# Output tiles of one stage in other buffers, a block's pools in another order, and its TensorE work in program order

## The chip, the cores and the metric

One core of a Trainium2 chip runs the kernel. The metric is device time in microseconds: 888.29 us, the median of three runs (886.44, 888.29 and 888.67 us).

TensorE (PE) does the matmuls; their weights are loaded on a second row of the profile (PEld). VectorE is DVE, ScalarE is ACT, GpSimd is POOL, SyncE is SP. Matmuls write PSUM, which has eight banks; DVE and ACT read them. SP issues nearly all DMAs, ACT issues a few. Each engine runs its instructions in the order in which the program holds them, and an instruction that waits holds up those behind it on its engine.

## The reference

An attention with 4 batches, 8 heads, 576 positions and head dimension 64 (half of the heads see a local window of 32, half see positions of the same residue modulo 32) gives 2304 rows of 512. Two feed-forward layers follow:

```python
h = x @ w_in                      # 2304 x 512 by 512 x 2048
x = (h - np.tanh(h)) @ w_out      # 2048 x 512
xn = x / np.sqrt(np.mean(x * x, axis=-1, keepdims=True) + 1e-06) * rms_g
g = xn @ w_gate                   # 512 x 1536
silu = g * (1.0 / (1.0 + np.exp(-g)))
return (silu * (xn @ w_val)) @ w_out   # 1536 x 512
```

The weights come as 8-byte floats, activations as 4-byte floats.

## The kernel before, in words

Every matmul operand is held as a high and a low part in TensorE's rounded 32-bit format, so a product takes three matmuls (high by high, high by low, low by high).

**Weights.** A raw tile (128 x 512 of 8-byte floats, 512 KB) is loaded by SP (L175). ACT reads it twice (L184 into a `ct` tile, L186 into a `ca` tile), DVE merges the two (L196), ACT writes the high part (L203) and DVE the low part (L207). `Stream.step` loads ahead, converts weight i and splits weight i - 1. For the second layer `Store.plain` (L343) and `Store.to` (L362) also put the merged and the split weights back to DRAM, since a later stage reads them again.

**First layer.** The 2304 rows run in five groups of columns; the last group (g = 4) has 512. For each of 16 slices f of the hidden dimension `unit` issues the 12 matmuls of h, tanh (ACT, L854), h - tanh (DVE, L859), the high part of g (ACT, L865), its low part (DVE, L870) and, one or two slices later, the 12 matmuls of the output (`pe_x`) into four PSUM banks. The tiles `tg` and `g` rotate through three buffers each; there are 82 units in all, so the last unit's g lies in `g0` and the one two before it in `g1`. After the last slice `evac_x` scales the four banks by ACT (L890) and stores them to the DRAM tensor `x2d` (L896); in the last group ACT issues the stores, two to a bank, and the tiles are `tg` buffers.

**Between the layers.** `preps` reads `x2d` back, takes the mean square (TensorE sums it with a matrix of ones, ps_r), computes the reciprocal root on DVE (L999 to L1010) and scales (L1013); `conv` (L1027, L1046, L1047) makes the seven operands of a Strassen product. It is a generator, drawn three steps at a time by the last group and by the plain block.

**The plain block.** The first 256 rows of the second layer are computed in the plain way, while the last weights are still being converted. For each f of 12 (L1376 to L1387): the stream is moved on, the stores of earlier weights are issued, `pe_gv` does 12 matmuls of 256 columns for gate and 12 for val, ACT takes the Silu (L937), DVE multiplies (L938), ACT and DVE split the product (L940, L941), and `pe_o` does the six matmuls with w_out2 for f - 2. Gate uses two PSUM banks in turn, val two others, and every third f uses two of the banks of `ps_x`, where the first layer's last output stood. The weights of out2 are ready in DRAM (L166).

**The Strassen stage** follows for the other 2048 rows, two blocks of 1024 by six pairs of f. Each pair does seven products for gate and val, and `out` (L1163). Its first product stands in the program before the plain block's last `pe_o` (L1123 to L1125, L1395).

**What sets the order.** A planner orders each engine's instructions by priority, which is the place in the program unless `high_priority` raises it, and by its own estimate of when an instruction is ready. Inside `manual_schedule` the named engines keep the order of the program. SP keeps it from near the end of group 3 (L1309). TensorE keeps it in groups 1 to 3 (L1298, L1311), is free in the last group and the plain block, and keeps it again from L1391.

**Pools.** A pool is placed on top of the pools that are open. Per partition, the region of `poolA` holds `cvt` (ca and ct, 8 KB), `held` (12 slots of 4 KB for weights), `gp` (tg, 6 KB) and `ghl` (g, 12 KB), 74 KB in all. When it closes, `pbn` takes 40 KB from its start and the pools of `poolB` lie above. On the other side `poolR` (the read-back x of the first 256 rows, the root's temporaries s2 and rz, and `ct2`) closes at the same time, and above poolA's old region there is some free space and then the place of `poolR`. The four pools of `poolB` need 16, 12, 12 and 9 KB (tmp, cvt2, rawb, pb), 49 in all: 34 lie in the rest of poolA's region and 15 above it. With `reuse_waits="tile"` a new tile waits for the last users of just those old tiles that it overlaps.

Of the kernel before, what the change touches and what calls it, by code (L numbers as in the profile page):

```python
# [7 lines left out]
F32 = mybir.dt.float32  # L8
# [12 lines left out]
WS = 2.0 ** -8  # L21
# [13 lines left out]
def attn_moe_moe_kernel(  # L35
# [24 lines left out]
    nc = tc.nc  # L60
    B, _, NC, D = q_str.shape
# [4 lines left out]
    S = NC * W  # L66
# [3 lines left out]
    SUB = 256  # L70
    subs = [[(b, t + 64 * u) for u in range(4)] for t in (0, SUB) for b in range(B)]
    subs[B:B] = [[(b, 2 * SUB) for b in range(B)]]
    groups = [(0, 1), (2, 3), (4,), (5, 6), (7, 8)]
    width = [SUB * len(g) for g in groups]
    NG = len(groups)
# [5 lines left out]
    def runs(s):  # L81

        r = []
        for i, (b, t) in enumerate(subs[s]):
            if r and r[-1][0] == b and r[-1][1] + r[-1][2] == t:
                r[-1][2] += 64
            else:
                r.append([b, t, 64, 64 * i])
        return r
# [23 lines left out]
    cvt = poolA.enter_context(tc.tile_pool(name="cvt", bufs=2))  # L113
    held = poolA.enter_context(tc.tile_pool(name="held", bufs=HELD))
    gp = poolA.enter_context(tc.tile_pool(name="gp", bufs=1))
    ghl = poolA.enter_context(tc.tile_pool(name="ghl", bufs=1))
# [9 lines left out]
    for s in range(len(subs)):  # L126
        if len(runs(s)) > 1 or s in LANES:
            _, t0, n, _ = runs(s)[0]
            sc[t0] = one.tile([128, n // W, (t0 + n) // W], F32, name=f"sc{t0}")

    x2d = dram.tile([DM, NT], F32, name="x2d")
# [3 lines left out]
    def nth(tag, n):  # L135

        turn[tag] = (turn.get(tag, -1) + 1) % n
        return f"{tag}{turn[tag]}"
# [192 lines left out]
    xt, tmp = {}, [wts, None, None, None]  # L331

    class Store:


        n = m = 0
# [546 lines left out]
            evac_x(g)  # L883

    def evac_x(g):
        queue = nc.sync if g < NG - 1 else nc.scalar
        for c in range(4):
            pool, tag = (gp, nth("tg", 3)) if g == NG - 1 else (cvt, ("ca", "ct")[c % 2])
            t = pool.tile([128, 512], F32, tag=tag, name="xe")[:, :width[g]]
            nc.scalar.mul(out=t, in_=xacc[g][c][:, :width[g]], mul=WS)  # L890
            for k, j in enumerate(groups[g]):
                dst, src = x2d[c * 128:c * 128 + 128, :], t[:, SUB * k:SUB * k + SUB]
                rs = runs(j)
                b, t0, n, _ = rs[0]
                if len(rs) == 1:
                    queue.dma_start(out=dst[:, b * S + t0:b * S + t0 + n], in_=src)  # L896
                else:
                    queue.dma_start(
                        out=dst.rearrange("p (b t) -> p b t", b=B)[:, :, t0:t0 + n],
                        in_=src.rearrange("p (b t) -> p b t", b=B),  # L900
                    )
# [21 lines left out]
    def pe_gv(j, f):  # L923
        r, n = [], R0
        for kd, pool, tag in (("gate", ps_h, "h"), ("val", ps_m, "m")):
            if f % 3 == 2:
                ps = bank_x("ps_" + tag)[:, :n]
            else:
                ps = pool.tile([128, 512], F32, tag=nth(tag, 2), name="ps_" + tag)[:, :n]
            w, x = w2[kd, f].t, xn[j]  # L930
            seq = [(a, e, c) for c in range(4) for a, e in ((0, 0), (0, 1), (1, 0))]
            for i, (a, e, c) in enumerate(seq):
                mm(ps, w[:, a, c, :], x[:, e, c, :], i == 0, i == len(seq) - 1)
            r.append(ps)
        with tc.high_priority(400):
            s = pb.tile([128, n], F32, tag="s", name="s", bufs=3)
            nc.scalar.activation(out=s, in_=r[0], func=ACTF.Silu, scale=WS)  # L937
            nc.vector.scalar_tensor_tensor(out=s, in0=r[1], scalar=WS, in1=s, op0=ALU.mult, op1=ALU.mult)  # L938
            t = pb.tile([128, 2, n], F32R, tag="p", name="p", bufs=3)
            nc.scalar.copy(out=t[:, 0], in_=s)  # L940
            nc.vector.tensor_tensor(out=t[:, 1], in0=s, in1=t[:, 0].bitcast(F32), op=ALU.subtract)  # L941
        p_of[j, f] = t
# [423 lines left out]
    for k, m in enumerate((3, 7)):  # L1366
        xt[m] = late[:, 2048 * k:2048 * k + 4 * HT].rearrange("p (e c t) -> p e c t", e=2, c=2)
    poolB = ExitStack()
    tmp[0] = poolB.enter_context(tc.tile_pool(name="tmp", bufs=4, reuse_waits="tile"))
    tmp[1] = None  # L1370
    cvt = poolB.enter_context(tc.tile_pool(name="cvt2", bufs=2, reuse_waits="tile"))
    tmp[2] = cvt
    tmp[3] = (poolB.enter_context(tc.tile_pool(name="rawb", bufs=3, reuse_waits="tile")), "raw")
    pb = poolB.enter_context(tc.tile_pool(name="pb", bufs=2, reuse_waits="tile"))

    for f in range(FB):  # L1376
        if f == FB - 4:
            pairs[0].fetch((0, 1))
        st2.to(max(3 * (f + 2), N1 + (len(w2_order) - N1) * (f + 1) // (FB - 2)))
        store.plain(st2.i - 1)  # L1380
        store.to(st2.i - 6)
        pe_gv(0, f)
        for _ in range(3 if f < FB - 2 else 40):
            next(pg, None)
        decode.to(max(0, min(8, 8 * (f - 4) // 6)))
        if f > 1:
            pe_o(0, f - 2)  # L1387
    pe_o(0, FB - 2)
    store.plain(len(w2_order))
    store.to(len(w2_order))  # L1390
    ctx.enter_context(tc.manual_schedule(engines={mybir.EngineType.PE, mybir.EngineType.SP}))  # L1391

    def second():
# [149 lines left out]
```

## Time and profile before

| | |
|---|---|
| median of three runs | 888.29 us (886.44 to 888.67) |
| the profiled execution | 887.14 us |
| its span, first to last instruction | 885.3 us |
| mean granted TensorE clock | 0.99 of full speed |
| TensorE busy | 865.6 us, 98% |
| DVE busy | 626.1 us, 71% |
| ACT busy | 413.7 us, 47% |
| the last group's output leaves PSUM | 463.4 to 468.7 us |
| the plain block's last out2 products end | 523.4 us |

A busy share is a mean over stages with different limits. The stretch that the change touches is read in time order, from 455 to 525 us. In a timeline row the first two numbers are the start and the time in us, `x` is how many instructions are merged, and the bracket says how long the engine stood idle before and what it waited for.

### The profile page before, as it was taken

How to read it: one execution, taken by the hardware profiler on the slowest of the kernel's cores; microseconds unless marked ns; L12 is line 12 of the kernel's file. 1: busy time of each engine (PE TensorE's matmuls, PEld its weight loads, DVE VectorE, ACT ScalarE, POOL GpSimd, SP SyncE). 2: the span in 40 equal slices, each digit the busy share in tenths (PEclk: the TensorE clock that was granted, in tenths of full speed). 3: DMA queues.
4: the chain of work that ended last, by engine and by line, in shares of the span. 5: the costliest groups of instructions: out<-in, count | busy, mean ns of one | idle time of the engine just before them, and what ended most of it. 6: DMA issues, size and time to landing. Idle time of an engine off the chain costs nothing.

```text
span 885.3 us, 14070 instructions
## 1 busy us (share of the span) xinstructions
PE 865.6 (98%) x5091; PEld 723.4 (82%) x5091; DVE 626.1 (71%) x1290; ACT 413.7 (47%) x916; POOL 247.6 (28%) x309
## 2 busy tenths in 40 slices
PE   7999999999999999999997999999999999999998
PEld 4888888888998887888887977888888888888886
DVE  5999778888779887657779845469688553435544
ACT  6887633323543333778657544533325324322230
POOL 0000057694366853000000449956200000000000
PEclk7999999999999999999999999999999999999999
DMA  9965224221313000889976889866661289544002
GB/s 302 367 221 180 76 75 157 98 63 36 116 55 110 25 19 26 330 311 366 412 262 226 302 304 410 329 239 214 212 216 48 82 315 348 182 147 140 1 1 95
DMA packets 63749, 164.12 MB, mean 185 GB/s; under 512 B 10112, under 2 KB 21760, under 8 KB 63680
## 3 DMA queue, kind: packets, MB, share of 16 engines
q1 hardware_dynamic: 62528, 162.18, 52.2%
q10 hardware_dynamic: 1152, 1.05, 0.3%
q8 instruction: 40, 0.66, 0.3%
q14 instruction: 29, 0.24, 0.1%
HBM read 119.16 MB, written 44.04 MB: 184 GB/s over the span
## 4 chain that ended last, share of the span: by engine, by line
PE 60%; DVE 9%; POOL 7%; issue 2%; DMA 2%; ACT 1%; ACTq 0%; SPq 0%; DVEq 0%; POOLq 0%
PE ps_pr L150 21%; PE ps_o L150 15%; PE ps_x L150 9%; PE ps_h L150 9%; POOL pr L674 5%; DVE so L714 4%; PE ps_q L150 4%; PE ps_m L150 1%; POOL pr L707 1%; DMA raw<-in_w_val_dram 1%; DVE tg L859 1%; DVE g L870 1%; DMA x2d<-xe 1%; DVE sm L450 0%; DMA sq<-in_q_str_dram 0%
## 5 line engine op out<-in xcount | busy, mean ns | idle before, releaser
L150 PE MATMUL ps_h<-xs,w 128*128 128x512 f32 (+1 forms) x984 | 214.3, 366 | 0.7 <-DVE tg L859 0.7
L150 PE MATMUL ps_x<-g,w 128*128 128x512 f32 (+1 forms) x984 | 214.1, 366 | 0.0
L150 PEld LDWEIGHTS ps_h<-xs,w 128*128 128x128 f32 x984 | 169.7, 190 | 30.5 <-DVE tg L859 1.2
L150 PEld LDWEIGHTS ps_x<-g,w 128*128 128x128 f32 x984 | 168.5, 189 | 30.3 <-ACT g L865 0.4
L150 PE MATMUL ps_pr<-xt,wt 128*128 128x512 f32 x576 | 137.0, 390 | 0.5 <-DVE s L1096 0.5
L150 PE MATMUL ps_o<-wt,p 128*128 128x512 f32 x576 | 135.9, 389 | 0.0
L150 PEld LDWEIGHTS ps_pr<-xt,wt 128*128 128x128 f32 x576 | 107.9, 188 | 23.6 <-DVE s L1096 0.9
L150 PEld LDWEIGHTS ps_o<-wt,p 128*128 128x128 f32 x576 | 108.1, 188 | 22.4
L674 POOL TENSOR_TENSOR pr<-sk,sq 128x256 f32<-128x256 f32 (+2 forms) x101 | 83.1, 857 | 132.2 <-DMA sq<-in_q_str_dram 127.8
L865 ACT CAST g<-tg 128x512 fp32r<-128x512 f32 (+1 forms) x82 | 46.5, 567 | 101.2 <-DVE tg L859 100.9
L1117 ACT COPY u<-ps_pr 128x512 f32<-128x512 f32 x72 | 41.9, 587 | 102.8 <-PE ps_pr L150 102.8
L707 POOL TENSOR_TENSOR pr<-sv,se 128x288 f32<-128x288 f32 (+12 forms) x104 | 69.7, 691 | 57.4 <-DVE so L714 19.8
L1169 DVE SCALAR_TENSOR_TENSOR osum<-ps_o,osum 128x512 f32<-128x512 f32 x80 | 54.8, 687 | 26.6 <-PE ps_o L150 25.9
L714 DVE TENSOR_REDUCE so<-pr 128x16 f32<-128x272 f32 (+11 forms) x104 | 64.8, 651 | 8.9 <-POOL pr L707 8.6
L302 POOL TENSOR_TENSOR ws<-wa 128x256 f32<-128x256 f32 x24 | 20.4, 872 | 179.6 <-DVE w L207 155.6
L150 PE MATMUL ps_pr<-xt,wo 128*128 128x512 f32 x288 | 67.4, 389 | 0.0
L150 PEld LDWEIGHTS ps_pr<-xt,wo 128*128 128x128 f32 x288 | 54.1, 188 | 11.2
L870 DVE TENSOR_TENSOR g<-tg,g 128x512 fp32r<-128x512 f32 (+1 forms) x82 | 55.2, 674 | 10.4 <-ACT g L865 9.8
L859 DVE SCALAR_TENSOR_TENSOR tg<-ps_h,tg 128x512 f32<-128x512 f32 (+1 forms) x82 | 50.5, 617 | 15.8 <-ACT tg L854 15.8
L196 DVE SCALAR_TENSOR_TENSOR ct<-ca,ct 128x512 uint32<-128x512 uint32 x68 | 47.5, 706 | 18.9 <-ACT ca L186 18.4
L854 ACT ACTIVATE tg<-ps_h 128x512 f32<-128x512 f32 (+1 forms) x82 | 44.2, 540 | 35.5 <-PE ps_h L150 35.4
L679 DVE TENSOR_REDUCE sc<-pr 128x4 f32<-128x256 f32 (+2 forms) x101 | 43.7, 436 | 12.1 <-POOL pr L674 11.6
(123 smaller groups left out, 1041.1 us busy)
## 6 DMA issues: line engine op xcount, KB each, us to landing
wt<-w SPq DMA_DIRECT2D x84, 512.0 KB, 4.6
w<-w SPq DMA_DIRECT2D x36, 512.0 KB, 6.2
raw<-in_w_out_dram SPq DMA_DIRECT2D x28, 512.0 KB, 6.1
w<-wo SPq DMA_DIRECT2D x24, 512.0 KB, 7.1
raw<-in_w_in_dram SPq DMA_DIRECT2D x16, 512.0 KB, 9.2
raw<-in_w_gate_dram SPq DMA_DIRECT2D x12, 512.0 KB, 7.0
raw<-in_w_val_dram SPq DMA_DIRECT2D x12, 512.0 KB, 7.4
v<-ct SPq DMA_DIRECT2D x24, 256.0 KB, 5.3
```

The lines of the kernel that those rows point to most:

```text
L150: nc.tensor.matmul(out_, lhsT, rhs, start=start, stop=stop, skip_group_check=True)
L196: nc.vector.scalar_tensor_tensor(out=t, in0=self.a.bitcast(U32), scalar=3, in1=t, op0=ALU.logical_shift_left, op1=ALU.bitwise_or)
L674: nc.gpsimd.tensor_tensor(out=pr, in0=self.k[:, a:e, :], in1=self.q[:, c - c0:c - c0 + 1, :].to_broadcast([128, e - a, D]), op=ALU.mult,)
L679: pend.append(lambda: nc.vector.tensor_reduce(out=s[:, c - c0, a:e], in_=pr, axis=AX.X, op=ALU.add))
L707: nc.gpsimd.tensor_tensor(out=pr, in0=self.v[:, 0:c + 1, a:e], in1=self.e[:, c - c0, 0:c + 1].unsqueeze(2).to_broadcast([128, c + 1, e - a ...
L714: pend.append(lambda: nc.vector.tensor_reduce(out=o[:, c - g0, a:e], in_=pr.rearrange("l c d -> l d c"), axis=AX.X, op=ALU.add))
L854: nc.scalar.activation(out=t, in_=h_of[g, f, a], func=ACTF.Tanh, scale=WS)
L859: nc.vector.scalar_tensor_tensor(out=t, in0=h_of.pop((g, f, a)), scalar=WS, in1=t, op0=ALU.mult, op1=ALU.subtract)
L865: nc.scalar.copy(out=t[:, 0], in_=t_of[g, f, a])
L870: nc.vector.tensor_tensor(out=t[:, 1], in0=t_of.pop((g, f, a)), in1=t[:, 0].bitcast(F32), op=ALU.subtract)
L1117: nc.scalar.copy(out=u, in_=x[kd])
L1169: nc.vector.scalar_tensor_tensor(out=o, in0=ps, scalar=WS, in1=o, op0=ALU.mult, op1=ALU.add)
```

## The change

In the last group `evac_x` scales the four banks into two tiles with the tags g0 and g1, two banks to a tile, and issues one store for each half of the columns and each tile: four stores of 256 KB in place of eight of 128 KB. The pools of `poolB` are opened in the order rawb, tmp, pb, cvt2 in place of tmp, cvt2, rawb, pb. From f = 3 of the plain block TensorE keeps the order of the program; this ends after the block's loop, where the existing block for TensorE and SP begins.

```diff
--- before.py
+++ after.py
@@ -883,19 +883,27 @@
             evac_x(g)
 
     def evac_x(g):
-        queue = nc.sync if g < NG - 1 else nc.scalar
+        if g == NG - 1:
+            for h in range(2):
+                t = ghl.tile([128, 2, 512], F32, tag=("g0", "g1")[h], name="xe")
+                for c in range(2):
+                    nc.scalar.mul(out=t[:, c], in_=xacc[g][2 * h + c], mul=WS)
+                for k, j in enumerate(groups[g]):
+                    b, t0, n, _ = runs(j)[0]
+                    dst = x2d[256 * h:256 * h + 256, b * S + t0:b * S + t0 + n].rearrange("(c p) t -> p c t", p=128)
+                    nc.scalar.dma_start(out=dst, in_=t[:, :, SUB * k:SUB * k + SUB])
+            return
         for c in range(4):
-            pool, tag = (gp, nth("tg", 3)) if g == NG - 1 else (cvt, ("ca", "ct")[c % 2])
-            t = pool.tile([128, 512], F32, tag=tag, name="xe")[:, :width[g]]
+            t = cvt.tile([128, 512], F32, tag=("ca", "ct")[c % 2], name="xe")[:, :width[g]]
             nc.scalar.mul(out=t, in_=xacc[g][c][:, :width[g]], mul=WS)
             for k, j in enumerate(groups[g]):
                 dst, src = x2d[c * 128:c * 128 + 128, :], t[:, SUB * k:SUB * k + SUB]
                 rs = runs(j)
                 b, t0, n, _ = rs[0]
                 if len(rs) == 1:
-                    queue.dma_start(out=dst[:, b * S + t0:b * S + t0 + n], in_=src)
+                    nc.sync.dma_start(out=dst[:, b * S + t0:b * S + t0 + n], in_=src)
                 else:
-                    queue.dma_start(
+                    nc.sync.dma_start(
                         out=dst.rearrange("p (b t) -> p b t", b=B)[:, :, t0:t0 + n],
                         in_=src.rearrange("p (b t) -> p b t", b=B),
                     )
@@ -1366,12 +1374,12 @@
     for k, m in enumerate((3, 7)):
         xt[m] = late[:, 2048 * k:2048 * k + 4 * HT].rearrange("p (e c t) -> p e c t", e=2, c=2)
     poolB = ExitStack()
+    tmp[3] = (poolB.enter_context(tc.tile_pool(name="rawb", bufs=3, reuse_waits="tile")), "raw")
     tmp[0] = poolB.enter_context(tc.tile_pool(name="tmp", bufs=4, reuse_waits="tile"))
+    pb = poolB.enter_context(tc.tile_pool(name="pb", bufs=2, reuse_waits="tile"))
+    cvt = poolB.enter_context(tc.tile_pool(name="cvt2", bufs=2, reuse_waits="tile"))
     tmp[1] = None
-    cvt = poolB.enter_context(tc.tile_pool(name="cvt2", bufs=2, reuse_waits="tile"))
     tmp[2] = cvt
-    tmp[3] = (poolB.enter_context(tc.tile_pool(name="rawb", bufs=3, reuse_waits="tile")), "raw")
-    pb = poolB.enter_context(tc.tile_pool(name="pb", bufs=2, reuse_waits="tile"))
 
     for f in range(FB):
         if f == FB - 4:
@@ -1379,6 +1387,9 @@
         st2.to(max(3 * (f + 2), N1 + (len(w2_order) - N1) * (f + 1) // (FB - 2)))
         store.plain(st2.i - 1)
         store.to(st2.i - 6)
+        if f == 3:
+            order = ctx.enter_context(ExitStack())
+            order.enter_context(tc.manual_schedule(engines={mybir.EngineType.PE}))
         pe_gv(0, f)
         for _ in range(3 if f < FB - 2 else 40):
             next(pg, None)
@@ -1388,6 +1399,7 @@
     pe_o(0, FB - 2)
     store.plain(len(w2_order))
     store.to(len(w2_order))
+    order.close()
     ctx.enter_context(tc.manual_schedule(engines={mybir.EngineType.PE, mybir.EngineType.SP}))
 
     def second():
```

## Rows read from the trace of the kernel before

**Rows 1.** The page, part 1: busy us, share of the span, instructions.

```profile
PE 865.6 (98%) x5091; PEld 723.4 (82%) x5091; DVE 626.1 (71%) x1290; ACT 413.7 (47%) x916; POOL 247.6 (28%) x309
```

**Rows 2.** TensorE's waits: line waited for, total us, times, longest us.

```profile
PE ps_h L150 <- ACT s L937: 4.9, 1, 4.9
PE ps_s L150 <- DMA dq<-in_near_d_dram: 1.5, 1, 1.5
...
PE ps_pr L150 <- DVE s L1096: 0.5, 1, 0.5
```

**Rows 3.** Timeline, TensorE, 455 to 495 us.

```profile
461.59 2.91 PE L150 MATMUL ps_x<-g,w 128*128 128x512 f32 x12
...
466.47 3.04 PE L150 MATMUL ps_m<-xn,w 128*128 128x256 f32 x24
...
474.45 4.45 PE L150 MATMUL ps_h<-xn,w 128*128 128x256 f32 x24 [4.94 <-ACT s L937]
```

**Rows 4.** Timeline, ACT and its DMA issues, 455 to 495 us.

```profile
463.40 1.09 ACT L890 ACTIVATE xe<-ps_x 128x512 f32<-128x512 f32 x2 [3.29 <-PE ps_x L150]
...
465.24 0.69 ACT L998 ACTIVATE acc<-ps_r,cole 128x512 f32<-128x512 f32 x1 [0.26 <-PE ps_r L150]
465.30 2.79 ACTq L896 DMA_DIRECT2D x2d<-xe  x4
...
468.13 0.60 ACT L890 ACTIVATE xe<-ps_x 128x512 f32<-128x512 f32 x1 [2.21 <-DMA x2d<-xe]
...
472.16 0.76 ACT L184 ACTIVATE ct<-raw,colf 128x512 uint32<-128x512 uint16 x1 [3.43 <-DMA x2d<-xe]
...
474.03 0.90 ACT L937 ACTIVATE s<-ps_h 128x256 f32<-128x256 f32 x3
```

**Rows 5.** Windows of 2 us: busy by engine, granted clock (PEclk), DMA.

```profile
474.00:476.00 2.00, 1.55 (x7) 1.55 (x8) 2.00 (x6) 2.00 (x6) 0.00 (x0) 0.51 0.16 59
476.00:478.00 2.00, 2.00 (x13) 2.00 (x13) 1.77 (x3) 2.00 (x4) 0.00 (x0) 0.63 0.20 76
478.00:480.00 2.00, 2.00 (x19) 2.00 (x18) 2.00 (x2) 2.00 (x3) 0.00 (x0) 1.00 0.87 272
```

**Rows 6.** Window of 25 us: the same columns.

```profile
475.00:500.00 25.00, 25.00 (x174) 23.75 (x173) 24.77 (x39) 21.08 (x38) 1.05 (x2) 0.95 0.78 265
```

**Rows 7.** Timeline, SP's DMA issues, 455 to 546 us.

```profile
474.87 3.05 SPq L343 DMA_DIRECT2D v<-ct  x2
...
508.13 0.39 SPq L175 DMA_DIRECT2D raw<-in_w_val_dram  x1
```

**Rows 8.** Timeline, TensorE and ACT, 494 to 546 us.

```profile
505.85 1.53 PE L150 MATMUL ps_x<-w,p 128*128 128x512 f32 x6
...
513.51 1.52 PE L150 MATMUL ps_pr<-xt,wt 128*128 128x512 f32 x6
...
515.33 1.60 PE L150 MATMUL ps_h<-xn,w 128*128 128x256 f32 x12
515.87 0.77 ACT L184 ACTIVATE ct<-raw,colf 128x512 uint32<-128x512 uint16 x1 [3.22 <-DMA raw<-in_w_val_dram]
...
516.76 1.55 PE L150 MATMUL ps_pr<-xt,wt 128*128 128x512 f32 x6
...
518.62 0.51 PE L150 MATMUL ps_m<-xn,w 128*128 128x256 f32 x2 [0.32 <-ACT w L203]
...
521.76 1.65 PE L150 MATMUL ps_x<-w,p 128*128 128x512 f32 x6 [0.95 <-ACT p L940]
```

**Rows 9.** The tile xe: ns of one issue, min/median/max.

```profile
L896 ACTq DMA_DIRECT2D x2d<-xe x8: 326/368/692, 464.0 to 469.1; - x8
L898 SPq DMA_DIRECT2D x2d<-xe x4: 583/616/1657, 279.9 to 282.9; - x4
```

**Rows 10.** DMA issues: count, KB, median us to landing.

```profile
x2d<-xe ACTq DMA_DIRECT2D x8, 128.0 KB, 3.6
```

**Rows 11.** Timeline, DVE, 455 to 495 us.

```profile
465.96 0.43 DVE L999 TENSOR_SCALAR sq<-acc 128x512 int32<-128x512 int32 x1 [5.12 <-ACT acc L998]
```

## Prediction

> **What bounds the kernel now.** I read the busy shares first: TensorE is busy for 865.6 of 885.3 us [rows 1], so no edit here can win more than the idle time that it removes, some 20 us in all, and the clock that goes with it. Then the list of TensorE's waits over the whole run, longest first: one wait of 4.9 us for ACT's Silu (L937) stands alone, the next is 1.5 us, and the only one listed for the Strassen products that follow is 0.5 us [rows 2]. Then the same place in order of time. TensorE ends the last group's output matmuls at 464.5, runs on into the plain block, ends the third pair of gate and val products at 469.5 and stands until 474.45, because the bank that it needs next is read by the first Silu [rows 3]. ACT shows why the Silu is late: it scales the four accumulators of the last group into three tg buffers, so the fourth waits 2.21 us for the first output DMA to land; it issues all eight output DMAs itself; and the conversion at 472.16 waits 3.43 us more, because its tile lies where the tg buffers were [rows 4]. The Silu follows at 474.03.
>
> The 2 us windows show a second cost of the same stop: the granted clock is 0.51 and 0.63 of full speed in the two windows after it and 1.00 again from 478 [rows 5]. The busy time of those windows, 1.55 and 2.00 us, at those shares, is a loss of 0.76 + 0.74 = 1.5 us.
>
> The other half of the block has another limit. The weights pass through a ring: SP loads a raw tile, ACT and DVE convert it, SP stores the result and only then comes to the next load. From 475 to 500 DVE is busy for 24.77 of 25 us and ACT for 21.08 [rows 6]. The last raw tile (val, f = 11) is loaded at 508.13, ACT gets it at 515.87, TensorE runs its products from 518.62, and the block's last out2 products end at 521.76 + 1.65 = 523.4 [rows 7, 8]. TensorE was kept busy up to there by work taken out of order: the first Strassen product (12 matmuls, at 513.51 and 516.76) goes before val 11, though it comes after it in the program [rows 8].
>
> **The change part by part.** The sum is made against the profiled execution, 885.3 us of span and 887.14 us in all, 1.15 us under the median of 888.29; I subtract the same microseconds from the median.
>
> *Output tiles.* Four ACT scalings stay. They go into g0 and g1, two to a buffer, so the wait of 2.21 us goes [rows 4]. g0 holds the last unit's g (82 units, three buffers, so the last is g0), and all twelve matmuls of that unit read it: the scaling of c = 0 can start at 464.5 instead of 463.40, 1.1 us later [rows 3, 4]. Four scalings at 0.55 us end at 466.7. Eight DMA issues on ACT's queue become four. Four of the old ones stand in one row of 2.79 us, 0.70 each with what lies between them [rows 4]; the issue alone is 326 to 692 ns, median 368 [rows 9]. A new one covers 256 rows of DRAM instead of 128. So four take 1.5 us at the old median, 2.8 at the 0.70; the nearest row of a larger pattern, the four-run store of the middle group (median 616 ns) [rows 9], says 2.5, and I take that. With 0.7 us for the norm's scaling, which stands among them now too, ACT is through at 464.5 + 2.2 + 0.7 + 2.5 = 469.9, and the last pair is issued between 468 and then.
>
> *The pools.* By the sizes, the region that closes holds ca/ct 8 KB, held 48, tg 6, g 12. Before, the plain block's ct and ca tiles began on tg; now rawb takes three slots of held, the temporaries take held's last slot, tg, g0 and half of g1, pb (the Silu's s and p) takes the rest of g1, g2 and free space, and ct/ca lie on the right side's closed pools. So the conversion that waited 3.43 us waits for no output DMA. But two of the three s tiles lie on g1, so a Silu can wait for the second output pair to land. The landing takes 3.6 us in the median on that queue [rows 10]: issued at 468 to 469.9, it has landed at 471.6 to 473.5. If the first s tile is the one on g2 it waits for nothing and the Silu runs at about 469.8. Ends: the stop of 4.94 us goes nearly whole, or only 474.03 - 473.5 = 0.5 us of it does. I take 472.0 for the Silu, 2.0 us before 474.03, nearer the landing rows, because the tiles of a pool are taken in turn and the lowest is on g1. The conversions that stood ahead of the Silu (472.16 to 474.03, 1.9 us) can run in that wait. TensorE started 0.4 us after the Silu did [rows 3, 4]; so the stop ends at 472.4 and shrinks by 2.0 us. I take 2.2, since four fewer transfers share the queue.
>
> *The clock.* A stop of 2.7 us instead of 4.94 brings back between nothing and all of the 1.5 us [rows 5]; I take half, 0.8.
>
> *Program order from f = 3.* It adds no instruction. It takes away TensorE's freedom to fill a wait. In order, val 11 is followed by two out2 steps (f = 9 and 10), the first Strassen product and out2 of f = 11. By their rows, val takes 1.6 us, an out2 step of six 1.5, the twelve Strassen matmuls 3.1: after val 11's weight arrives 1.6 + 1.5 + 1.5 + 3.1 + 1.5 = 9.2 us, against 523.4 - 518.6 = 4.8 us now [rows 8]; less 0.15 us of overlap per step, 8.5. So the order costs 3.7 us if TensorE still waits for that weight, 0.6 if the Strassen product may still go ahead (its own block of program order did pass unordered work before), and nothing if the weights come 3.7 us sooner. What can bring them: SP stood behind the stop too; its first store of the block waited until 474.87, and the later loads stand behind it [rows 7]. With the first conversion 2 to 4 us sooner that store can go at 471 to 473. Against it: DVE idles 5.12 us before 465.96, which the change doesn't touch, and has no gap from there to 500 [rows 6, 11]. I take the ring to gain what the order loses, net nothing, with -2 and +3.7 as ends.
>
> The Trainium skill, "TensorE: Matmul & The Clock Gate", section "Loop structure matters more than you think", speaks against this part: whether the array stays at full clock depends on whether the program makes it wait between bursts. The trace agrees: after the one stop the windows show 0.51 and 0.63. By that rule an in-order wait as long as today's stop would take back 1.5 us of clock beside its own length, and the sum would be 1.5 us instead of 3.0.
>
> Sum: 2.2 + 0.8 + 0 = 3.0 us. On the profiled execution 884.1, on the median 885.3. After 523 TensorE has almost no idle time [rows 2], so I let the gain stand to the end.
>
> **The rivals.** *A, the forecast*: 885.3.
>
> *B, the ring hides it*: the stop shrinks, but val 11 still arrives at 518 because DVE is full, and TensorE waits there instead; the Strassen product may go ahead. For it: DVE's 24.77 of 25 us, and ACT's wait of 3.22 us for the last load [rows 6, 8]. Against it: ACT and SP were idle behind the stop, so some links move. Time: 888.3 + 0.6, less 1 us if the ring moves by half of the Silu's 2 us: 887.9.
>
> *C, the order blocks the end*: program order puts out2 9 and 10 and the Strassen product behind val 11. Price 3.7 us, and up to 1.5 us of clock if the wait before it is as long as today's stop; it decides if the ring gains less than about 1 us. Time 888.3 + 3.7 = 892, with the front's gain swallowed by the wait. For it: the fill at 513.51 and 516.76 [rows 8]. Against it: one front gain of 2 us in the ring halves it.
>
> *D, the pools don't free the Silu*: its s tile waits for the second pair up to 473.5. Then 0.5 us is won and the rest is as in B: 887.8. It goes with B.
>
> *E, the whole stop goes* and the ring follows: 4.94 + 1.5 = 6.4 us, 881.9. It goes with the faster side.
>
> **How the numbers follow.** About 0.3%, 2.7 us, is what can be told from no change. A and E together 0.42, of which E 0.10; B and D 0.31; C 0.27. A by itself lies between 883.5 and 887, so part of it could not be told from no change (under 885.6 it could); about as much of B falls under that line, so I leave faster 0.42, same 0.31, slower 0.27. The likeliest case gives 885.3. The range that holds 8 in 10 reaches from E's side, 881.8, to C, 892.
>
> **What would show it.** The step on the output tiles: four scalings back to back after 464.5, no wait between them for an output DMA, four issues under 0.75 us each. The pools: no conversion that waits for an output DMA, and the first Silu at about 472; at 469.8 E is right, after 473 D. The clock: one window or none under 0.9 after the stop. The order: the first Strassen product after val 11 or before it; TensorE's waits for w (L203, L207) between 500 and 520, under 1 us in all for A, over 3 us for C. The ring: the load of the last raw tile before 506 for A, at 507 to 508 for B. The prediction is wrong if the block's last out2 products end later than 523.4, or if TensorE's stop at 469.5 is as long as before.

## The result: slower, and the profile after

The changed kernel takes 893.85 us (median of 7 runs, 892.12 to 897.8) against 888.4 us before (7 runs, 886.44 to 889.3): ratio 1.0070, 95% interval 1.0047 to 1.0093, so it is slower by 0.5 to 0.9%. Forecast was 885.3, range 881.8 to 892.0. Some executions of e2, e4, e8 and e9 below, and one of the kernel before beside e9 to e11, took 1440 us and more; medians and ratios leave them out, and the profiled executions of e8 and e9 were such ones, so the table of the runs has no row for these two.

The profiled execution took 896.41 us, span 894.6 (before 887.14 and 885.3). So the two profiles lie 9.3 us apart and the medians 5.45: the profiled execution after is one of the slower ones of its kernel (mean granted clock 0.985; the fastest, 892.12 us, had 0.992), and what is read off the pair is more than the usual loss. Behind the edit of the output tiles every line number is 8 higher, so the Silu is L945.

The whole run's TensorE waits, to be read against [rows 2] (line waited for, total us, times, longest us): the Silu's wait is shorter, as foreseen, and a second one, for DVE's half of p, is new.

```profile
PE ps_x L150 <- DVE p L949: 3.7, 1, 3.7
PE ps_h L150 <- ACT s L945: 3.4, 1, 3.4
...
PE ps_pr L150 <- DVE s L1104: 1.1, 1, 1.1
```

ACT's timeline after, against [rows 4]. The output tiles did what was forecast: four scalings in a row, four issues. Then ACT stands 5.75 us at the Silu, whose tile lies on g1, until the output has landed, and the first conversion, which waits for nothing, comes behind it and three more Silus at 476.88 (before: 472.16).

```profile
464.56 2.31 ACT L890 ACTIVATE xe<-ps_x 128x512 f32<-128x512 f32 x4 [3.74 <-PE ps_x L150]
466.42 0.39 ACTq L894 DMA_DIRECT2D x2d<-xe  x1
...
466.84 1.60 ACTq L894 DMA_DIRECT2D x2d<-xe  x3
473.20 0.94 ACT L945 ACTIVATE s<-ps_h 128x256 f32<-128x256 f32 x3 [5.75 <-DMA x2d<-xe]
...
476.88 0.76 ACT L184 ACTIVATE ct<-raw,colf 128x512 uint32<-128x512 uint16 x1
```

SP's timeline, against [rows 7]: the ring's first store is 8.1 us later, its last raw load 5.6 (0.7 of it because all that lies ahead ended 0.7 later).

```profile
482.93 2.06 SPq L343 DMA_DIRECT2D v<-ct  x2
...
513.77 0.43 SPq L175 DMA_DIRECT2D raw<-in_w_val_dram  x1
```

TensorE's timeline, against [rows 3] and [rows 8]: two stops, val 11 at 524.21 instead of 518.62, and 18 out2 matmuls behind it instead of 6, ending at 526.23 + 4.27 = 530.50 (before 523.41). The Strassen product at 518.55 did go ahead of gate 11.

```profile
473.63 2.93 PE L150 MATMUL ps_h<-xn,w 128*128 128x256 f32 x12 [3.42 <-ACT s L945]
...
497.52 2.08 PE L150 MATMUL ps_x<-w,p 128*128 128x512 f32 x4 [3.72 <-DVE p L949]
...
518.55 1.63 PE L150 MATMUL ps_pr<-xt,wt 128*128 128x512 f32 x6 [0.37 <-DMA wt<-w]
...
524.21 0.51 PE L150 MATMUL ps_m<-xn,w 128*128 128x256 f32 x2
...
526.23 4.27 PE L150 MATMUL ps_x<-w,p 128*128 128x512 f32 x18
```

The 2 us windows, against [rows 5], columns as there (window, length, PE, PEld, DVE, ACT, POOL busy, granted clock, DMA): around the end of each stop stand four windows with a granted clock of 0.50 to 0.74. Busy time times what is missing of the clock gives 2.7 us for either set, 5.5 in all; before it was 1.5.

```profile
472.00:474.00 2.00, 0.37 (x1) 0.37 (x2) 0.39 (x2) 0.80 (x3) 0.00 (x0) 0.58 0.31 108
474.00:476.00 2.00, 2.00 (x11) 2.00 (x11) 2.00 (x7) 1.14 (x4) 0.00 (x0) 0.50 0.00 0
476.00:478.00 2.00, 2.00 (x11) 2.00 (x11) 0.90 (x2) 1.40 (x3) 0.00 (x0) 0.50 0.00 0
478.00:480.00 2.00, 2.00 (x11) 1.83 (x10) 0.77 (x2) 1.42 (x3) 0.00 (x0) 0.71 0.00 0
496.00:498.00 2.00, 0.48 (x1) 0.48 (x2) 2.00 (x4) 0.75 (x3) 0.00 (x0) 0.56 1.02 355
498.00:500.00 2.00, 2.00 (x7) 1.61 (x7) 2.00 (x5) 0.86 (x2) 0.00 (x0) 0.50 0.77 272
500.00:502.00 2.00, 2.00 (x12) 2.00 (x11) 2.00 (x4) 1.74 (x3) 0.00 (x0) 0.50 1.01 345
502.00:504.00 2.00, 2.00 (x14) 2.00 (x14) 2.00 (x4) 1.89 (x4) 0.00 (x0) 0.74 0.71 231
```

TensorE's second stop, of 3.72 us, is a wait for DVE, which does 2.35 us of preparations ahead of p's low part:

```profile
494.78 2.35 DVE L1055 TENSOR_TENSOR xt<-tr,xt 128x1024 fp32r<-128x1024 f32 x2
497.05 0.42 DVE L949 TENSOR_TENSOR p<-s,p 128x256 fp32r<-128x256 f32 x1
```

DVE, which was full from 465.96 to 500 before [rows 6, 11], now stands 2.07 us for the Silu and 2.33 us for val's matmuls, which TensorE runs at half clock. The first merge of a weight comes at 482.22 (before: 474.16), though its conversion was done at 477.53 + 0.67 = 478.20: the waiting product and the chain's four scalings stand ahead of it.

```profile
473.61 1.09 DVE L946 SCALAR_TENSOR_TENSOR s<-ps_m,s 128x256 f32<-128x256 f32 x3 [2.07 <-ACT s L945]
...
479.23 0.42 DVE L946 SCALAR_TENSOR_TENSOR s<-ps_m,s 128x256 f32<-128x256 f32 x1 [2.33 <-PE ps_m L150]
...
482.22 0.69 DVE L196 SCALAR_TENSOR_TENSOR ct<-ca,ct 128x512 uint32<-128x512 uint32 x1
```

The same 15 us from the end of the output matmuls, DVE alone (window, length, busy, clock, DMA), first after, then before (464 to 479): 4.6 us less work done.

```profile
465.00:470.00 5.00, 2.42 (x4) 1.00 0.58 138
470.00:475.00 5.00, 2.86 (x7) 0.73 0.49 177
475.00:480.00 5.00, 2.67 (x7) 0.58 0.00 0
sum 15.00, DVE 7.95; mean DVE 2.65
```

```profile
sum 15.00, DVE 12.54; mean DVE 4.18
```

Where the 9.3 us between the two profiled spans lie: 0.7 ahead of the block, 6.4 in it (from the start of the last output matmul, 464.81 against 464.11, to the end of the last out2: 65.7 against 59.3), 2.0 behind it and 0.2 after the last matmul. The start is chance: over all runs below that matmul starts between 461.1 and 465.1, as TensorE stands and loses clock by different amounts in the stages before it. So only times from it on are compared. Of the 6.4, 1.95 is more standing (gaps between matmuls 8.38 against 6.43) and the other 4.4 the same 342 matmuls run slower (4.0 of it by the clock, 5.5 against 1.5). The medians being 5.45 apart, these shares are those of this pair and not of every execution.

### The profile page after: what moved, and what is told of

The parts are those of the page before. It is cut to its first block, busy times and chain, and to the rows that moved or that the text cites. A ratio compares the mean times of both kernels' runs of the same rounds, so it can differ in the third digit from the quotient of the medians.

```text
span 894.6 us, 14061 instructions
## 1 busy us (share of the span) xinstructions
PE 869.8 (97%) x5091; PEld 725.8 (81%) x5091; DVE 628.8 (70%) x1290; ACT 413.8 (46%) x916; POOL 245.0 (27%) x309
## 4 chain that ended last, share of the span: by engine, by line
PE 71%; DVE 12%; POOL 7%; DMA 4%; issue 3%; ACT 2%; SPq 1%; ACTq 0%; DVEq 0%; POOLq 0%
PE ps_pr L150 20%; PE ps_h L150 16%; PE ps_x L150 15%; PE ps_o L150 14%; POOL pr L674 5%; DVE so L714 4%; PE ps_q L150 4%; DMA raw<-in_w_in_dram 1%; DMA raw<-in_w_gate_dram 1%; POOL pr L707 1%; PE ps_v L150 1%; PE ps_s L150 1%; PE ps_p L482 1%; DVE tg L859 1%; DVE g L870 1%
## 5 line engine op out<-in xcount | busy, mean ns | idle before, releaser
L707 POOL TENSOR_TENSOR pr<-sv,se 128x288 f32<-128x288 f32 (+12 forms) x104 | 70.2, 695 | 56.3 <-DVE so L714 19.8
L1177 DVE SCALAR_TENSOR_TENSOR osum<-ps_o,osum 128x512 f32<-128x512 f32 x80 | 54.8, 687 | 26.9 <-PE ps_o L150 26.3
L870 DVE TENSOR_TENSOR g<-tg,g 128x512 fp32r<-128x512 f32 (+1 forms) x82 | 55.3, 675 | 10.8 <-ACT g L865 9.6
L679 DVE TENSOR_REDUCE sc<-pr 128x4 f32<-128x256 f32 (+2 forms) x101 | 43.7, 437 | 12.1 <-POOL pr L674 11.6
```

The source lines that it names most:

```text
L679: pend.append(lambda: nc.vector.tensor_reduce(out=s[:, c - c0, a:e], in_=pr, axis=AX.X, op=ALU.add))
L707: nc.gpsimd.tensor_tensor(out=pr, in0=self.v[:, 0:c + 1, a:e], in1=self.e[:, c - c0, 0:c + 1].unsqueeze(2).to_broadcast([128, c + 1, e - a ...
L870: nc.vector.tensor_tensor(out=t[:, 1], in0=t_of.pop((g, f, a)), in1=t[:, 0].bitcast(F32), op=ALU.subtract)
L1177: nc.vector.scalar_tensor_tensor(out=o, in0=ps, scalar=WS, in1=o, op0=ALU.mult, op1=ALU.add)
```

## The experiments

Theory 1: the pools put a wait for the output's landing at the head of ACT's queue, and the conversions stand behind it, so the ring runs late. Theory 2: program order on TensorE costs by itself. The times of the block in each profiled run, read from the timelines, in us behind the start of the last output matmul (last two columns: length of the block, and from its end to the last matmul). Each row is one execution, and a difference of a microsecond or two may be chance: the profiled execution of e6 (890.89) lies 5.0 us under its kernel's median, that of e13 (884.28) 3.9 under, that of the changed kernel 2.6 over.

| run | first conversion | first Silu | last weight's high part | val 11 | block | behind it |
|---|---|---|---|---|---|---|
| before | 8.1 | 9.9 | 53.8 | 54.5 | 59.3 | 358.3 |
| after | 12.1 | 8.4 | 58.7 | 59.4 | 65.7 | 360.3 |
| e1 tiles, pools | 13.8 | 8.4 | 58.7 | 59.4 | 66.2 | 360.0 |
| e2 order | 7.0 | 8.8 | 51.9 | 56.7 | 65.2 | 358.0 |
| e3 pools | 8.7 | 0.7 | 56.8 | 57.5 | 62.3 | 360.4 |
| e4 tiles | 3.7 | 11.5 | 49.1 | 52.6 | 61.0 | 360.3 |
| e5 | 3.7 | 9.4 | 53.5 | 57.8 | 62.0 | 360.4 |
| e6 (order) | 3.7 | 9.4 | 52.8 | 57.9 | 66.3 | 357.8 |
| e7 order from 6 | 7.2 | 9.0 | 53.4 | 54.7 | 60.4 | 359.6 |
| e10 | 2.5 | 5.0 | 52.2 | 56.3 | 60.6 | 359.9 |
| e11 (order) | 3.7 | 6.1 | 53.0 | 58.3 | 66.9 | 359.2 |
| e12 | 7.0 | 8.8 | 53.6 | 54.8 | 59.4 | 360.3 |
| e13 | 2.5 | 5.0 | 51.0 | 53.7 | 57.9 | 358.8 |
| e14 (order) | 11.3 | 8.5 | 59.5 | 60.1 | 68.7 | 360.2 |
| e15 | 8.7 | 0.7 | 54.0 | 55.3 | 60.5 | 359.3 |
| e16 | 8.3 | 1.1 | 60.1 | 61.0 | 65.5 | 360.0 |
| e17 | 1.9 | 7.3 | 53.1 | 53.8 | 58.9 | 359.3 |
| e18 (order) | 1.9 | 8.6 | 53.5 | 56.6 | 62.3 | 359.4 |

**The parts alone.** The kernel before with one or two hunks of the change's diff: e1 the output tiles and the pools, e2 the order, e3 the pools, e4 the output tiles.

> The change without the program order on TensorE: output tiles and pools as changed, TensorE free. Theory 1 (the first Silu's tile lies on g1, so ACT waits for the output DMA with the weight conversions queued behind it, and the weight ring starts late): almost the whole loss stays, 4 to 6 us slower than before; ACT's wait for the output DMA about 5.7 us, SP's first merged-weight store of the block about 8 us later than before. Theory 2 (program order on TensorE is what costs): within 1 us of before, or faster.

> Only the program order on TensorE from f = 3; tiles and pools as before. Theory 1: the ring starts as before (first store near 475), the last weight arrives as before, and the end of the block is at most 1.5 us later: 0 to 2 us slower. Theory 2: 4 to 6 us slower, with TensorE waits of several us between 490 and 520.

> Only the pools in the new order; the output tiles stay in tg with eight stores, TensorE free. The first Silu's tile lies on g1, which no output uses now. Theory 1: the Silu waits for no output DMA, TensorE's stop of 4.9 us shrinks to under 1 us, and the ring starts no later than before: 1 to 4 us faster. Theory 2 says nothing against it: 0 to 3 us faster. A third possibility, that the new places of the conversion tiles alone delay the ring: 2 to 5 us slower.

> Only the output tiles through g0 and g1 with four stores; pools and TensorE's freedom as before. Conversion tiles lie on tg, which no output uses now, except one on g0; the Silu's tile lies on the closed pools of the other side. Theory 1: no long wait of ACT for an output DMA ahead of the first conversion, which starts by 469; ring 3 to 4 us earlier; 1 to 4 us faster. Theory 2: 0 to 3 us faster. If half the stores change nothing: within 1 us.

Measured, with the kernel before at 887.27 beside them: e1 894.36, ratio 1.0077 (1.0048 to 1.0106); e2 892.22, 1.0055 (1.0037 to 1.0072); e3 891.32, 1.0042 (1.0021 to 1.0062); e4 890.96, 1.0033 (1.0014 to 1.0052). Tiles and pools without the order have the whole loss, as Theory 1 said; the order alone nearly has it too, as Theory 2 said of its size; they don't add up. And e3 and e4, which both theories had faster, are slower (for e3 only the third possibility, the new places of the conversion tiles, had named such a time). In e4 the conversions go first and the last weight comes 4.7 us earlier than before, but the Silu runs 1.5 us later behind them and the first stop grows:

```profile
473.15 5.01 PE L150 MATMUL ps_h<-xn,w 128*128 128x256 f32 x24 [6.47 <-ACT s L945]
```

In e3 the Silu runs at once and TensorE has no first stop at all. The 4.94 us come back as waits, most of them in the last third of the block, with the last weight 3.0 us later; conversions now stand behind second-round Silus (the third conversion at 15.8 us, before 11.3):

```profile
506.10 1.20 PE L150 MATMUL ps_x<-w,p 128*128 128x512 f32 x4 [2.09 <-ACT p L940]
...
521.44 0.50 PE L150 MATMUL ps_m<-xn,w 128*128 128x256 f32 x2 [1.71 <-ACT w L203]
```

In e2 TensorE, beside a first stop of 3.8 us, does not wait for weights at all but stands in order for p, 2.0 and 3.4 us (earlier than the 490 to 520 expected), and the windows from 480 to 488 have a granted clock of 0.69 and then 0.50:

```profile
479.96 1.42 PE L150 MATMUL ps_x<-w,p 128*128 128x512 f32 x4 [2.04 <-ACT p L940]
484.78 3.78 PE L150 MATMUL ps_x<-w,p 128*128 128x512 f32 x8 [3.41 <-DVE p L941]
```

**Two lines exchanged.** e5 is e1, e6 the changed kernel, both with

```diff
     tmp[3] = (poolB.enter_context(tc.tile_pool(name="rawb", ...)), "raw")
+    pb = poolB.enter_context(tc.tile_pool(name="pb", ...))
     tmp[0] = poolB.enter_context(tc.tile_pool(name="tmp", ...))
-    pb = poolB.enter_context(tc.tile_pool(name="pb", ...))
     cvt = poolB.enter_context(tc.tile_pool(name="cvt2", ...))
```

so that no Silu tile lies on an output; e8 has the same four pools and the old output tiles; e7 is the kernel before with `if f == 3` of the order's hunk made `if f == 6`.

> Output tiles and pools as in the change, but the activation pool stands second (raw, pb, tmp, cvt2), so that the first Silu's tile lies on a slot no output leaves from; TensorE free. Theory 1 (what costs is ScalarE's in-order queue: the Silu and the first weight conversions must both go by about 4 to 7 us after the output scalings, and each variant so far delays one of the two): the first conversion comes as early as with the output tiles alone (464.9), the Silu right behind four conversions (about 467.5), TensorE stops 1 to 2 us instead of 4.9 and the weight loads run 5 to 7 us ahead of those of before; the block from the last pe_x to the last pe_o takes 54 to 56 us (before 59.3), in all 882 to 885. Rival 3 (the loss of every variant is the 2 us that all with new tiles or pools lost after the block, and block time does not reach the end): the block is shorter and the time stays at 888 to 891.

> The changed kernel with two lines exchanged: the activation pool ahead of the scratch pool; TensorE in program order as in the change. Theory 1 with the cost of order resting on a late start of the weight conversions: 884 to 888, waits of TensorE for p under 2 us in all. Theory 2 (program order costs by itself, 4.9 us as in the run with the order alone): 889 to 893, with waits of TensorE for p of 4 us or more in 475 to 500 and a lower granted clock behind them.

> The kernel before with TensorE in program order from f = 6 on instead of f = 3, nothing else. If the order's cost is made in its first stints, where ScalarE and VectorE still catch up on conversions and TensorE stops for p (5.5 us of stops in 478 to 488 in the run with the order alone): 886.5 to 889. If it is made over the whole block or at its end: 891 to 893.

> The kernel before with its plain block's pools in the order raw, pb, tmp, cvt2 and the old output tiles; TensorE free. Theory 1: the last output scaling still waits for the first tile's landing (468), then four conversions, then the Silu near 472: TensorE stops about 3 us instead of 4.9, the loads start 2 to 3 us earlier than before: 884.5 to 887. Rival 3: 888 to 891, as with the other order of the pools.

Before 887.67; e5 890.7, 1.0041 (1.0025 to 1.0057); e6 895.87, 1.0097 (1.0072 to 1.0122); e7 888.51, 1.0019 (1.0007 to 1.0031); e8 889.2, 1.0023 (1.0011 to 1.0035). e5 and e8 miss Theory 1's ranges and lie in Rival 3's, though not for its reason, since the block of e5 is not shorter than before. From e1 to e5 the last weight comes 5.2 us earlier, the block shrinks by 4.2 and the ratio falls from 1.0077 to 1.0041 (3.2 us): Theory 1 holds for that part. The kernel is still not fast: one conversion went early, then ACT met the next wait at its head, a tile on the rms chain's rz, with the Silu behind it:

```profile
472.03 0.76 ACT L184 ACTIVATE ct<-raw,colf 128x512 uint32<-128x512 uint16 x1 [3.22 <-DVE sq L1018]
```

e7 shows where the order costs: begun at f = 6 it costs 1.7 us by its ratio (0.6 to 2.8) in place of 4.9 (3.3 to 6.4), so most of the loss is made in the first stints, where TensorE in order waits for p. e6 has that loss undiminished (a stop of 5.4 us for p) and lies above both ranges given for it. Against the changed kernel it speaks against Theory 1 as a full account: the last weight comes 5.9 us earlier, and the time is no better (1.0097 against 1.0070). The order adds 5 us to e5 (to give e6) and nothing to e1 (to give the changed kernel). So in the changed kernel neither taking away the order alone (e1) nor moving the pool alone (e6) gives anything back; both together do (e5).

**ACT's queue freed.** e9 is e5 with, in `pe_gv` and `Weight.scale`,

```diff
-            s = pb.tile([128, n], F32, tag="s", name="s", bufs=3)
+            s = pb.tile([128, n + 104], F32, tag="s", name="s", bufs=3)[:, :n]
...
+            self.a = cvt.tile([128, 512], F32, tag="ca", name="ca")
             w = self.raw.rearrange("p c f -> p (c f)").bitcast(U32)...
...
-            self.a = cvt.tile([128, 512], F32, tag="ca", name="ca")
```

e10 also issues the last group's outputs by `nc.sync.dma_start`; e11 is e9 with the order.

> As the run with the activation pool second (output tiles changed, pools raw, pb, tmp, cvt2, TensorE free), but the Silu tiles are 104 columns longer and a conversion's two tiles are allotted in the other order, so that the first two conversions lie neither on the output tiles nor on the rms chain's rz, for which ScalarE stood 3.2 us in that run. Theory 1 (ScalarE's queue must have no wait at its head after the output scalings): four conversions from 3.7 us behind the last pe_x, the Silu at 6.4, TensorE stops about 1.3 us (it runs dry at 5.4) instead of 4.5 to 6.5 and hardly falls in clock, loads 5 us ahead of before; the block takes 55 to 57 us (before 59.3), in all 883.5 to 886.5 with 2 us lost behind the block, else 882 to 884. Rival 4 (what is taken from the first stop returns later in the block as waits for p or weights, as in the run with the pools alone): block 59 to 62 us, in all 888 to 891.

> The same with the last group's four output transfers issued from SyncE's queue instead of ScalarE's. ScalarE saves about 2 us of issues: conversions from 1.7 us behind the last pe_x, the Silu at 4.5, before TensorE runs dry at 5.4, so no first stop and no fall in clock. Theory 1: 0.5 to 2 us faster than with the issues on ScalarE: 882 to 885.5. Rival 4: the same 888 to 891 as there.

> The changed kernel (TensorE in program order from f = 3) with the same three edits of placement. Theory 1 alone: within 2 us of the run without the order, 884 to 888. Theory 2 (order costs also with ScalarE's queue free, since TensorE then waits for p in place of going ahead): 889 to 893, with stops for p of 4 us or more in all and the clock at about half of full speed behind them.

Before 887.2; e9 889.75, 1.0025 (1.0013 to 1.0038); e10 888.78, 1.0014 (1.0002 to 1.0026); e11 894.72, 1.0074 (1.0060 to 1.0088). e9 and e10 lie where Rival 4 had such times, e11 above both its ranges. ACT did run as designed in e10 (conversions at 2.5, Silu at 5.0 us), and TensorE stood as long as ever, for another engine: DVE multiplies the first Silu only behind the rms chain and its four scalings.

```profile
475.41 4.38 PE L150 MATMUL ps_m<-xn,w 128*128 128x256 f32 x24 [5.14 <-DVE s L946]
```

Theory 1 was too narrow: a wait at ACT's head is harmful, but taking it away here only hands the stop to DVE. Theory 5: DVE's backlog sets the pace.

**DVE's work put later.** The draws of `preps` in the plain block (e12: the kernel before; e13: e10; e14: the changed kernel; e15: e3):

```diff
-        for _ in range(3 if f < FB - 2 else 40):
+        for _ in range((0 if f < 4 else 1) if f < 8 else 40):
```

> The kernel before, with the preparations of the Strassen operand handed out later: none for f under 4, one for each f from 4 to 7, the rest from f = 8 (before: three for each f). Theory 5 (VectorE's backlog in the first 35 us sets the weight ring's pace, and it the end): some 9 us of VectorE work go behind the weight merges and splits; the last weights come 3 to 5 us earlier, the three end waits of 1.5 us vanish, the first stop of 4.9 us stays: block 57 to 58.5 us (before 59.3), in all 885 to 887. Theory 1 alone (ScalarE's head waits): no change, 886.5 to 889.

> The run with ScalarE's queue free and the output transfers on SyncE, with the preparations late. There TensorE's first stop had moved to a wait of 5.1 us for VectorE's multiply of the first Silu behind the rms chain; that wait stays within 1 us, later waits (1.4 and 1.0 us) go: theory 5: block 57.5 to 59.5 (60.6 there), in all 885 to 887.5. Without it: 888 to 890.

> The changed kernel with the preparations late, nothing else. Its ring runs 5 us late since VectorE stood idle 5 us of the first 15 us. Theory 5: VectorE makes these good out of the 9 us of preparations that go behind: the weights come 4 to 6 us earlier, TensorE's wait for p of 3.7 us in 493 to 498 shrinks to under 1 us and the clock's second fall with it; the block takes 58 to 61.5 us in place of 65.7, in all 886 to 890. Theory 2 (program order costs by itself): 892 to 895 as before.

> The kernel before with the change's pools alone and the preparations late. With the pools alone the first stop was gone, but 7.5 us of waits came late in the block, since the weights ran 3 us later. Theory 5: the weights run 3 to 6 us earlier, most of the late waits go and none comes first: block 54 to 58 us, in all 882 to 886, faster than the kernel before. Without it: 890 to 892 as with the pools alone.

Before 888.17; e12 889.15, 1.0003 (0.9987 to 1.0018); e13 888.13, 0.9995 (0.9979 to 1.0011); e14 897.52, 1.0090 (1.0072 to 1.0107); e15 890.16, 1.0019 (1.0008 to 1.0030). None of the four times lies in Theory 5's range. Against e10 and e3 the blocks of e13 and e15 shrink by 2.6 and 1.8 us, the first as expected, the second by less than half of it, and the intervals of the ratios overlap in both pairs; e12 stays, and in e14 TensorE waits 7.9 us for val's weights from 43 us on, so that it is with e6 the slowest of all. So DVE's backlog is at most one limit, not the limit.

**The rms chain put later.** In the last group (e16: the kernel before; e17: e10; e18: the changed kernel):

```diff
-            for _ in range(0 if pg is None or f > 14 else 3):
+            for _ in range(0 if pg is None or f > 12 else 3):
```

> The kernel before, with the preparation's rms chain handed out later: the last group stops after f = 12 instead of 14, so that the rest comes in the plain block. If the chain's place ahead of the first Silu product is what holds VectorE and so TensorE: the Silu and its product come at once (TensorE's first stop 0 to 1.5 us instead of 4.9), block 55 to 58.5 us (before 59.3), in all 883 to 887. If the loss comes back later in the block (conversions still wait for the outputs' landing): 888 to 890.

> Output tiles changed and issued from SyncE, pools raw, pb, tmp, cvt2 with the longer Silu tiles and the exchanged allotment, TensorE free, and the rms chain late. ScalarE has no wait at its head and VectorE merges the first weights and the first products before the chain: no stop over 2 us, the third weight split 2 to 4 us earlier than before, block 53 to 57 us, in all 880 to 885, faster than both kernels. If the block is bound otherwise: 887 to 890.

> The changed kernel with the rms chain late; its planner then puts the first two conversions ahead of the first Silu, which still waits for the landing of the second output pair. Theory 1 (the loss is the ring, started late behind that Silu): conversions 10 us earlier, the last weights 4 us or more earlier, TensorE's first stop of 3.4 us stays: 887 to 891. Theory 2 (program order costs by itself, 4.9 us): 892 to 895.

Before 887.19; e16 894.46, 1.0070 (1.0046 to 1.0094); e17 889.3, 1.0028 (1.0011 to 1.0045); e18 891.94, 1.0040 (1.0017 to 1.0063). e18 is the cleanest test of Theory 1: in the changed kernel the planner now puts two conversions ahead of the waiting Silu. The Silu is as late as in the changed kernel, TensorE's first stop even longer (5.2 us), yet the last weight comes 5.2 us earlier and the block is 3.3 us shorter. The time, 891.94, lies between the two ranges, and the interval of its ratio overlaps that of the changed kernel, so the times alone do not bear the gain out. DVE does 10.7 us of work in the first 15 instead of 7.95:

```profile
sum 15.00, DVE 10.69; mean DVE 3.56
```

In e17 a ring that starts early wins nothing, and its trace shows where. Its first conversion is 6 us ahead of before, the clock does not fall in the block, and the last weight is nearly as late as before (53.1 us, before 53.8). The lead is lost on SP: four loads for the next stage stand there, 9.5 us of it for DVE's p, and the next raw load stands behind them until 497.20 (before 497.29). e17, then before:

```profile
485.60 11.56 SPq L291 DMA_DIRECT2D wa<-v  x4
497.20 0.43 SPq L175 DMA_DIRECT2D raw<-in_w_val_dram  x1
```

```profile
495.32 1.87 SPq L291 DMA_DIRECT2D wa<-v  x4
497.29 0.38 SPq L175 DMA_DIRECT2D raw<-in_w_val_dram  x1
```

e16 lies above both of its ranges, in the main for the same reason: the Silu runs at 1.1 us and TensorE has no first stop, but these four loads stand 11.48 us, 9.6 of it for DVE's s, the next raw load comes at 501.72, ACT waits 6.95 us for it and TensorE 4.6 for the weight.

No version beat the kernel before; e12 and e13 equal it.

## Why the prediction was wrong, step by step

- **Output tiles: right in kind.** No wait for an output DMA, issues of 2.0 us (2.5), ACT through at 468.4 (469.9). That the scalings begin at 464.56 (forecast 464.5) is luck: the whole stage ended 0.7 us later in this execution, and counted from the start of the last output matmul they begin 0.46 us later than before, not 1.1.
- **The pools: the step that failed.** The landing was seen, and the Silu at 473.2 is the late end of the range given for it. What failed is that "the conversions that stood ahead of the Silu" were to "run in that wait": the planner put them behind it, on an engine that takes its instructions in order. DVE did 4.6 us less work in that stretch, and the ring went off late; where the conversions go ahead again, the block is 4.2 us (e5 against e1) and 3.3 us (e18 against the changed kernel) shorter. It is not all of the loss: in e6 the ring is as early, and the order alone keeps the time up. The stop itself shrank by 1.5 us (2.2 forecast).
- **The clock: wrong sign.** 0.8 us was to come back; two stops of 3.4 and 3.7 us cost 5.5 us of clock instead of 1.5, so 4.0 were lost. The rule cited from the Trainium skill, "TensorE: Matmul & The Clock Gate", section "Loop structure matters more than you think", held for these two: the granted clock was 0.50 to 0.74 behind them. An in-order wait was priced there and given no weight in the sum; and the price was the clock alone, though the text says that the wait's own length comes beside it. With its 4.94 us the sum given there would have been a loss of 3.4 us and not a gain of 1.5.
- **Program order: the second step that failed.** It was to be repaid by a ring 3.7 us ahead; the ring was 5 us behind. And its price was looked for at the end alone. There it was small (6.3 us from val 11 to the end, 4.8 before; the Strassen product did go ahead); the larger part is a stop for p 29 us into the block, where DVE does preparations first. Alone it costs 4.9 us (e2), begun at f = 6 1.7 (e7).
- **"The gain stands to the end": wrong.** Behind the block another 2.0 us went, perhaps by chance; see the last section.
- **Rival C** named the nearest time, 892, with its condition (the ring gains under 1 us) met, but not its place: TensorE waited in the middle of the block, and its fill at the end survived. Rival B's thought, that a shorter stop is paid back by the ring, is what e3 and e17 show.

Behind all of it stands one reading error. The 4.94 us stop was taken for a loss to be won. TensorE, ACT, DVE and SP hold each other in this block: the wait removed on one (e3, e10, e16) returned on the next, a ring 4.7 us ahead (e4) was paid with a longer stop, while an engine idled early (after, e1) was never made good.

## What to carry to other kernels

A long wait in a list is worth its length only if every other queue of the stretch has slack behind it; where one engine is full, ask what it is given to do during the wait. When a tile moves onto memory that a DMA still reads, look at everything queued behind the instruction that will wait, not only at that instruction. And fix an engine's order only where its inputs are ahead: the same order cost 4.9 us from f = 3 and 1.7 from f = 6.

## What was not expected of the hardware

The length of a stop does not tell the clock's cost: 4.94 us before was followed by 1.5 us of loss [rows 5], 3.42 and 3.72 us after by 2.7 each, and in e17 a stop of 2.21 us by none. The granted clock also differs between executions of one kernel: the seven of the changed kernel have mean granted clocks of 0.983 (897.8 us) to 0.992 (892.12 us).

The 2.0 us behind the block follow no single edit: that stretch takes 357.8 to 360.4 us over the runs, 360.3 in e12, which changes neither tiles nor pools, and 357.8 in e6, which changes both. One half of it is seen. From 617 on the engines do the same work in the same order, but DVE's operations beside POOL's take longer than the same ones before, and the eviction that frees TensorE's bank comes 1 us late. DVE and POOL after, and the same operations before:

```profile
617.00 2.46 DVE L1021 SCALAR_TENSOR_TENSOR x<-x,gcol,acc 128x512 f32<-128x512 f32 x2
...
620.28 1.61 POOL L286 TENSOR_TENSOR wo<-ws,wo 128x512 fp32r<-128x512 f32 x1
620.67 1.77 DVE L1104 SCALAR_TENSOR_TENSOR s<-v,s 128x512 f32<-128x512 f32 x1
...
623.00 1.80 POOL L286 TENSOR_TENSOR wo<-ws,wo 128x512 fp32r<-128x512 f32 x1
623.57 1.78 DVE L1109 TENSOR_TENSOR p<-s,p 128x512 fp32r<-128x512 f32 x1
```

```profile
609.01 1.88 DVE L1013 SCALAR_TENSOR_TENSOR x<-x,gcol,acc 128x512 f32<-128x512 f32 x2
...
611.43 1.13 POOL L285 CAST wo<-ws 128x512 fp32r<-128x512 f32 x1
612.01 1.09 DVE L1096 SCALAR_TENSOR_TENSOR s<-v,s 128x512 f32<-128x512 f32 x1
```

In each of the three pairs POOL's operation began first and DVE's ended 0.54 or 0.55 us behind POOL's end (622.44 against 621.89, 625.35 against 624.80, 613.10 against 612.56): it looks as if DVE's waited for POOL's to end. So its length goes by which of POOL's operations it meets: the longer one (L286) after, the shorter (L285) before. The rule of the Trainium skill, "SBUF — State Buffer", section "SBUF: two separate sides", is that a VectorE operation with two inputs in that memory and a GpSimd operation that reads there exclude each other for a whole instruction; these rows agree. That this meeting moved is seen; that the edits moved it is not shown, since e12, without them, has the same two DVE operations at 1.78 us each and TensorE's waits behind them. What moves it stays open, as does the other half of the 2.0 us, waits for DVE between 537 and 550.
